# Block 1 of a retention layer computed as one chunk of 128 tokens, and no products of zeros

## The chip, the cores and the metric

The kernel runs on one core of a Trainium2 chip. The metric is the device time of one execution in microseconds (us), from three runs for the kernel before. All engine times below come from one profiled execution of that kernel.

## The reference, cut to what matters

The layer has two halves. The first is a retention (linear attention with decay) over batch 4, 8 heads, 768 tokens, head size 64, in blocks of 64 tokens. The second is a channel mix on the 512-wide result, with two weight matrices between 512 and 1024 and one gate of 512 by 512.

```python
for b in range(nb):                      # 12 blocks of 64 tokens
    intra = einsum('bhic,bhjc->bhij', qb, kb) * Dmask       # lam ** (i - j), lower triangle
    intra = einsum('bhij,bhjd->bhid', intra, vb)
    inter = einsum('bhid,bhde->bhie', qb * lam_pow, kv_state)
    out[:, :, sl] = intra + inter
    kv_state = lam_block * kv_state + einsum('bhsd,bhse->bhde', kb * rev_pow, vb)
...
xk = mu_k * x + (1 - mu_k) * x_prev ; xr = mu_r * x + (1 - mu_r) * x_prev
k = maximum(xk @ w_k, 0) ; v = k * k @ w_v ; r = sigmoid(xr @ w_r) ; return r * v
```

The block length is only a way of computing: a chunk of 128 tokens with the decay carried on gives the same numbers as two of 64.

## The kernel before, in words

The 768 tokens are cut into NT = 6 blocks of 128 (index n), and the 8 heads into HP = 4 pairs (index hp). Each step of the work is a two or three letter word, and the string `ORDER` lists all the words; every engine gets its instructions in that order, and no scheduler changes it. A word is a letter, the block and the pair (or part):

- `L` and `N` load the inputs of a block and pair on SP's queue, `M` clears the halves of the tile that must be zero (POOL). There are two input tiles, `in0` and `in1` (in_104 and in_105 where instructions are listed), for even and odd pairs, so a load waits until the pair two steps earlier has been read.
- `A` scores (PE, tile `sc`), `a` decay of the scores (DVE, into `mv`), `q` decay of the queries (DVE, also into `mv`), `k` decay of the keys (ACT), `U` sums of keys by values (PE, tile `u`), `u` and `w` the update of the state `st` (DVE, with copies by ACT), `B` values (PE, tile `xp`).
- `E`, `F`, `e`, `f` mix a token with the one before (ACT, POOL, DVE); `x`, `y` split the result in two parts (ACT, DVE); `R`, `Q` gate products (`rp`), `K` first products (`kp`), `h` and `p` square and split, `V` second products (`vp`), `s` and `o` outputs.
- `S`, `c`, `C`, `D` load a 64-bit weight matrix and turn it into 32-bit numbers (SP, ACT, POOL, DVE).
- `T` makes the tables of decay powers; `Z` followed by a count puts that many products of a zero tile on PE, into a PSUM tile `idle` that nobody reads.

Block 0 is one chunk of 128 tokens: no state is needed, 8 score products and 8 value products per pair. In every later block (n of 1 and more) each pair works on two chunks of 64, called even and odd (`eo`). There the score product has 128 rows in its stationary side, the two heads being separated by zeros, and the values are one product per head, batch and chunk: the 64 rows of values and the 64 rows of state stand on top of each other in one stationary tile, and decayed scores and decayed queries on top of each other in `mv`. That is why `to_values` copies the state into the input tile twice per pair, and why `decay_queries` writes four pieces.

In a matmul's row of the profile the two numbers with a star (128*64, 64*64) are the part of the TensorE array that it uses, rows by columns. A 32-bit product shows as two records.

Of the kernel before, what the change touches and what calls it, by code (L numbers as in the profile page):

```python
# [7 lines left out]
F32 = mybir.dt.float32  # L8
# [25 lines left out]
def tile_retention_moe(  # L34
    ctx: ExitStack,
    tc: tile.TileContext,
    qvk0: bass.AP,
# [50 lines left out]
    LP = const.tile([128, H, 64], F32, name="LP")  # L88
    LC = tiny.tile([128, HP], F32, name="LC")
# [3 lines left out]
    def load_hp(n, hp):  # L93
        t = IN[hp % 2]
        if n == 0:
            sync.dma_start(t[:, 0:4].rearrange("p c o -> p (c o)"), qvk0[hp])
            return
        sync.dma_start(t[:, 2:4].rearrange("p c o -> p (c o)"), kk[n - 1, hp])

    def load_qv(n, hp):  # L100
        t = IN[hp % 2]
        for i in range(2):
            rows, cols = slice(i * 64, i * 64 + 64), slice(i * 4, i * 4 + 2)
            sync.dma_start(t[rows, cols].rearrange("p c o -> p (c o)"), qv[n - 1, hp, rows])
# [3 lines left out]
    def clear(n, hp):  # L108
        t = IN[hp % 2]
        gpsimd.memset(t[64:128, 0 if n == 1 and hp < 2 else 1:2], 0.0)  # L110
        gpsimd.memset(t[0:64, 4 if n == 1 and hp < 2 else 5:6], 0.0)
# [6 lines left out]
    smalls = tiny.tile([128, 7 + H + 2 * HP], F32, name="smalls")  # L118
    sync.dma_start(smalls, small)
    rows = [work.tile([128, w], F32, tag="rt", name="rows", bufs=4) for w in (328, 200)]  # L120
    eye = rows[0][:, 200:328]
    sync.dma_start(rows[0], hot)
    lcol, ecol, lrow, erow, prow = (smalls[:, a:b] for a, b in ((0, 1), (1, 5), (5, 13), (13, 14), (14, 15)))
    mus = smalls[:, 7 + H:].rearrange("p (w c) -> p w c", w=2)
# [5 lines left out]
    zeros = work.tile([128, 1024], F32, tag="kf", name="zeros")  # L130
    vector.memset(zeros, 0.0)
    lone = work.tile([128, 640], F32, tag="kf", name="lone")
    gpsimd.memset(lone[:, 512:640], 1.0)
# [13 lines left out]
    rows = rows[1]  # L147
    vector.tensor_scalar(omu, mus, -1.0, 1.0, op0=ALU.mult, op1=ALU.add)
# [4 lines left out]
    idle = ps_m.tile([128, 512], F32, tag="m", name="idle")  # L153

    def powers(step):
        i = int(step[1])
        if i == 2:
            by_head = lone[:, 0:512].rearrange("p (h i) -> p h i", h=H)
            vector.tensor_tensor(by_head, rows[:, 72:136].rearrange("p (o i) -> p o i", o=1).broadcast_to([128, H, 64]),
                                 eye[:, 15::16].rearrange("p (h o) -> p h o", o=1).broadcast_to([128, H, 64]), op=ALU.mult)  # L160
            tensor.matmul(tables[2], lone[:, 512:640], lone[:, 0:512], start=True, stop=True)
            scalar.copy(LP.rearrange("p h i -> p (h i)"), tables[2])
            for ab in range(2):
                half = slice(ab * 64, ab * 64 + 64)
                gpsimd.tensor_copy(LC[half], LP[half, :, 63].rearrange("p (h a) -> p a h", a=2)[:, ab])
# [7 lines left out]
    zeros = zeros.bitcast(mybir.dt.bfloat16)  # L173

    def keep_busy(count):

        for _ in range(count):
            tensor.matmul(idle, zeros[:, 0:128], zeros[:, 512:1024], start=True, stop=True)
# [70 lines left out]
    def scores(n, hp):  # L249
        q = Q[hp % 2]  # L250
        if n == 0:
# [19 lines left out]
    def decay(n, hp):  # L271
        sc, mv = scs.pop((n, hp)), mv_of(n, hp)
        if n == 0:
# [14 lines left out]
    def decay_queries(n, hp):  # L288
        q, mv = Q[hp % 2], mv_of(n, hp)
        for eo in range(2):  # L290
            dr = slice(64, 128) if eo == 0 else slice(0, 64)
            for ab in range(2):
                rows = slice(ab * 64, ab * 64 + 64)
                lp = LP[rows, 2 * hp + ab:2 * hp + ab + 1, :].broadcast_to([64, B, 64])
                vector.tensor_tensor(mv[dr, eo, :, ab, :], q[rows, ab, :, eo, :], lp, op=ALU.mult)

    def decay_keys(n, hp):
        kn = KN[hp % 2]
        for ab in range(2):
            h = 2 * hp + ab  # L300
            scalar.activation(kn[:, :, ab, :], kn[:, :, ab, :], AF.Copy, scale=(PW if n == 0 else KD)[:, h:h + 1])

    def sums(n, hp):
        kn, vs = KN[hp % 2], VS[hp % 2]
        us[n, hp] = u = ps_1.tile([128, B, 2, 64], F32, tag="u", name="u")
        for b in range(B):
            for ab in range(2):
                if n == 0:
# [14 lines left out]

    def even_state(n, hp):
        u, state = us[n, hp][:, :, 0, :], ST[hp]
        if n == 0:
            scalar.copy(state, u)
            return
        to_values(n, hp, 0, state)
        vector.scalar_tensor_tensor(state, state, LC[:, hp:hp + 1], u, op0=ALU.mult, op1=ALU.add)  # L330
        to_values(n, hp, 1, state)

    def odd_state(n, hp):
        vector.scalar_tensor_tensor(ST[hp], ST[hp], LC[:, hp:hp + 1], us.pop((n, hp))[:, :, 1, :],
                                    op0=ALU.mult, op1=ALU.add)

    def values(n, hp):
# [146 lines left out]
Sr0 cr0 Cr0 Z10 T0 L00 Sr1 Z1 A00 k00 U00 a00 Z2 B00 cr1 L01 u00 Cr1 Sr2 k01 A01 a01 E00 U01 cr2 L02 u01 e00 T1 B01  # L484
Sr3 E01 L03 T2 F00 k02 Cr2 A02 f00 R00 e01 cr3 a02 U02 B02 M10 k03 u02 F01 f01 A03 Cr3 U03 Sk0 e02 R01 E02 a03 ck0 N10
L10 L11 Q00 f02 F02 R02 u03 Sk1 k10 q10 B03 N11 M11 Ck0 U10 E03 A10 Sk2 F03 Q01 R03 Q02 L12 e03 f03 ck1 u10 a10 B10
Sk3 N12 w10 Sv0 Sv1 M12 k11 U11 A11 s00 Ck1 Q03 s01 q11 E10 e10 ck2 k12 f10 u11 s02 K00 h00 a11 F10 A12 B11 M13 w11
L13 E11 Ck2 e11 a12 ck3 U12 K01 u12 f11 N13 K02 k13 s03 F11 Ck3 K03 w12 x10 cv0 A13 q12 B12 h01 h02 p00 h03 E12 N20
Sv2 Cv0 cv1 a13 L20 Dv0 U13 K04 u13 K05 Cv1 q13 K06 h04 p01 Dv1 K07 Sv3 M20 cv2 w13 A20 k20 U20 V00 h05 y10 L21 Cv2
k21 F12 e12 f12 V02 B13 h06 cv3 Dv2 M21 u20 Cv3 p02 N21 w20 h07 Dv3 p03 y11 x11 Dr0 V04 V06 q20 Dr1 U21 A21 V01 E13  # L490
V03 e13 V05 V07 o00 o01 a20 F13 f13 Dk0 B20 o02 o03 L22 y13 x12 R10 Q10 R11 Q11 R12 Q12 N22 u21 a21 x13 y12 Dk1 R13
Q13 L23 s10 q22 K10 s11 M22 E20 q21 K11 e20 s12 s13 w21 f20 F20 k22 U22 h10 A22 x20 Dk2 B21 K12 M23 a22 Dk3 K13 K14
h11 e21 N23 E21 F21 K15 h12 K16 p10 f21 h13 k23 u22 w22 B22 h14 U23 x21 A23 K17 p11 h15 E22 F22 u23 w23 V10 h16 y20
L30 p12 V12 a23 k30 V14 y21 e22 f22 M30 q23 h17 x22 L31 N30 A30 U30 p13 k31 B23 L32 V16 E23 V11 e23 a30 F23 u30 q30
N31 w30 V13 f23 M31 U31 y22 o10 B30 e30 u31 o11 A31 y23 k32 V15 o12 V17 R20 o13 E30 N32 q32 f30 x23 Q20 R21 Q21 R22
Q22 R23 L33 k33 Q23 q31 a31 M32 s20 w31 F30 s21 x30 B31 E31 e31 U32 F31 u32 w32 A32 a32 f31 M33 K20 s22 h20 L40 N33
K21 s23 B32 E32 F32 A33 x32 U33 h21 K22 u33 N40 q33 h22 L41 K23 h23 p20 k41 p21 K24 K25 h24 K26 K27 a33 h25 V20 k40
h26 p22 h27 y30 p23 w33 e32 f32 x31 V22 y31 V21 M40 B33 U40 A40 L42 M41 q40 e33 E33 f33 V24 u40 F33 N41 a40 w40 y32
V23 y33 B40 A41 o20 E40 U41 a41 F40 u41 V26 e40 L43 V25 V27 q41 x33 k42 o21 w41 o22 M42 f40 N42 A42 o23 B41 N43 U42
M43 L50 E41 a42 k43 u42 R30 F41 q42 w42 Q30 R31 Q31 R32 Q32 e41 R33 f41 Q33 x40 B42 s30 s31 U43 x41 A43 a43 E42 F42  # L500
q43 s32 s33 u43 w43 K30 N50 q50 x42 h30 K31 K32 h31 p30 K33 K34 h32 h33 p31 K35 h34 K36 h35 K37 L51 V30 h36 y40 e42
k50 y41 V32 V34 f42 h37 p33 p32 U50 B43 E43 A50 u50 V31 V33 y42 e43 N51 k51 F43 o30 f43 a50 q51 V35 V36 A51 U51 o31
B50 e50 a51 f50 o32 V37 E50 o33 u51 R40 Q40 F50 R41 Q41 B51 R42 Q42 x50 L52 k52 L53 x43 E51 F51 R43 y43 Q43 s40 N52
U52 N53 u52 q52 A53 s41 a53 s42 A52 K40 h40 q53 K41 h41 a52 s43 k53 K42 K43 h42 p40 K44 K45 K46 h43 h44 x51 p41 h45
e51 h46 f51 p42 K47 B52 h47 U53 y50 u53 p43 y51 V40 V42 e52 V41 E52 f52 V43 V44 F52 o40 y52 V46 V45 V47 B53 o41 o42
o43 x52 e53 f53 y53 R50 Q50 R51 Q51 R52 Q52 E53 F53 x53 R53 Q53 s50 s51 K50 K51 s52 h50 s53 h51 K52 h52 K53 h53 p51
p50 K54 h54 K55 h55 K56 K57 h56 h57 p53 V50 V52 V54 p52 V51 V53 o50 o51 V56 V55 V57 o52 o53
# [54 lines left out]
```

## Time and profile before

| what | us |
|---|---|
| median of three runs (lowest to highest) | 433.15 (430.15 to 433.55) |
| time of the profiled execution | 432.04 |
| its span from the first to the last instruction | 430.3 |
| PE busy in the span | 419.5 |
| DVE, ACT, POOL busy | 264.0, 204.9, 71.0 |
| PE's last product ends | 426.3 |

The time of the profiled execution is 1.74 us more than its span. A line of groups or of the timeline gives engine, operation, output and input tiles, the shape, a count behind an x, and in brackets the idle time of the engine ahead of it with what ended it. A line of the chain of waits gives a start, a length, and the engine that the end of the program can be traced back to in that time. A stretch of the windows view gives the busy time of each engine in it, the granted clock, the DMA share and GB/s.

### The profile page before, as it was taken

To read this page: it belongs to the slowest core of one execution; us is meant where nothing else is said; L and a number is where in the kernel's file an instruction comes from. 1 tells how busy PE (TensorE), PEld (TensorE's weight loads), DVE (VectorE), ACT (ScalarE), POOL (GpSimd) and SP (SyncE) were. 2 spreads that over 40 slices of the span, in tenths; PEclk is the share of its full clock that TensorE was granted. 3 is DMA by queue.
4 is the path that set the end of the run, shared out by engine and by line. 5 is a ranking of instruction groups with operands and counts; after the bars stand their busy time and mean duration, and the time that the engine had idled before them with its cause. 6 is when DMAs were issued, how large, how long until landed. Compare 5 with 4: busy or idle time off the path is not lost.

```text
span 430.3 us, 7314 instructions
## 1 busy us (share of the span) xinstructions
PE 419.5 (98%) x2935; PEld 328.9 (76%) x2935; DVE 264.0 (61%) x402; ACT 204.9 (48%) x357; POOL 71.0 (16%) x142
## 2 busy tenths in 40 slices
PE   7998899999999999999999999999999999999996
PEld 4665545668888888888888888888878888888885
DVE  5886999979867674746667646555437561414411
ACT  3645686586677643344644434454244460224300
POOL 4366554331102011110020200000000000000000
PEclk9999999999999999999999999999999999999999
DMA  7889918131403213515004523004520001100001
GB/s 295 304 308 330 300 48 277 66 97 50 146 3 99 87 46 107 153 58 140 0 2 131 187 78 99 0 0 123 161 62 0 2 1 50 50 2 0 0 30 69
DMA packets 12306, 42.60 MB, mean 99 GB/s; under 512 B 1776, under 2 KB 2160, under 8 KB 10736
## 3 DMA queue, kind: packets, MB, share of 16 engines
q1 hardware_dynamic: 8672, 35.84, 26.5%
q10 hardware_dynamic: 3600, 6.29, 4.0%
q8 instruction: 23, 0.38, 0.4%
q14 instruction: 11, 0.09, 0.1%
HBM read 35.83 MB, written 6.29 MB: 98 GB/s over the span
## 4 chain that ended last, share of the span: by engine, by line
PE 81%; DVE 7%; DMA 6%; ACT 2%; POOL 1%; issue 1%; SPq 0%; DVEq 0%; ACTq 0%
PE vp L30 29%; PE kp L30 26%; PE rp L30 13%; PE xp L30 5%; PE sc L30 4%; DMA wst<-w_k 4%; PE u L30 3%; DMA in<-qv 2%; DVE wst L30 2%; DVE mv L30 1%; DVE lov L30 1%; PE table L30 1%; ACT wu L30 1%; DVE wu L30 1%; POOL wu L30 1%
## 5 line engine op out<-in xcount | busy, mean ns | idle before, releaser
L30 PE MATMUL vp<-hiv,k 128*128 128x512 f32 (+1 forms) x400 | 122.8, 384 | 1.0 <-ACT kf L30 1.0
L30 PEld LDWEIGHTS vp<-hiv,k 128*128 128x128 f32 x400 | 74.1, 188 | 16.9 <-ACT kf L30 1.4
L30 PE MATMUL vp<-lov,k 128*128 128x512 f32 (+1 forms) x200 | 76.2, 381 | 0.0
L30 PE MATMUL kp<-xh,hik 128*128 128x512 f32 x160 | 62.9, 393 | 0.0
L30 PE MATMUL kp<-xl,hik 128*128 128x512 f32 x160 | 62.3, 389 | 0.0
L30 PE MATMUL kp<-xh,lok 128*128 128x512 f32 x160 | 62.3, 389 | 0.0
L30 ACT ACTIVATE ts<-xp,omu 128x512 f32<-128x512 f32 x48 | 31.8, 684 | 62.5 <-PE xp L30 44.2
L30 DVE TENSOR_TENSOR kf<-kp,kf 128x512 f32<-128x512 f32 x40 | 27.4, 688 | 37.2 <-ACT kf L30 37.1
L30 ACT ACTIVATE kf<-kp 128x512 f32<-128x512 f32 x48 | 28.4, 594 | 37.6 <-PE kp L30 37.2
L30 ACT COPY in<-st 64x256 f32<-64x256 f32 x80 | 32.3, 404 | 22.1 <-DVE st L30 17.8
L30 PEld LDWEIGHTS vp<-lov,k 128*128 128x128 f32 x200 | 37.6, 188 | 6.9
L30 DVE TENSOR_TENSOR mv<-sc,Dt 64x512 f32<-64x512 f32 (+1 forms) x48 | 32.6, 686 | 12.3 <-PE sc L30 11.9
L30 DVE TENSOR_TENSOR xl<-ts,xh 128x512 fp32r<-128x512 f32 x40 | 27.7, 703 | 19.3 <-ACT xh L30 19.2
L30 DVE SCALAR_TENSOR_TENSOR ts<-xp,smalls,ts 128x512 f32<-128x512 f32 x40 | 29.6, 747 | 15.8 <-ACT ts L30 15.6
L30 DVE TENSOR_TENSOR mv<-in,LP 64x256 f32<-64x256 f32 x80 | 34.5, 431 | 3.2 <-DMA in<-qv 1.6
L30 DVE TENSOR_TENSOR k<-kf,k 128x1024 fp32r<-128x1024 f32 x24 | 29.1, 1223 | 10.7 <-ACT k L30 10.7
L30 DVE TENSOR_TENSOR rt<-vp,rt 128x512 f32<-128x512 f32 (+1 forms) x25 | 16.4, 665 | 31.5 <-PE vp L30 31.2
L30 PEld LDWEIGHTS kp<-xh,hik 128*128 128x128 f32 x160 | 30.0, 188 | 7.0 <-issue 0.9
L30 PEld LDWEIGHTS kp<-xh,lok 128*128 128x128 f32 x160 | 30.0, 188 | 6.3
L30 PEld LDWEIGHTS kp<-xl,hik 128*128 128x128 f32 x160 | 30.0, 188 | 6.0
L30 ACT CAST xh<-ts 128x512 fp32r<-128x512 f32 x40 | 24.1, 616 | 21.7 <-DVE rt L30 18.2
L30 DVE SCALAR_TENSOR_TENSOR st<-st,LC,u 128x256 f32<-128x256 f32 x36 | 17.2, 478 | 24.8 <-ACT in L30 20.0
(70 smaller groups left out, 586.3 us busy)
## 6 DMA issues: line engine op xcount, KB each, us to landing
in<-qv SPq DMA_DIRECT2D x40, 256.0 KB, 4.5
in<-kk SPq DMA_DIRECT2D x20, 512.0 KB, 4.6
out<-rt ACTq DMA_DIRECT2D x23, 256.0 KB, 2.0
in<-qvk SPq DMA_DIRECT2D x4, 1024.0 KB, 6.3
wst<-w_k SPq DMA_DIRECT2D x4, 1024.0 KB, 9.2
wst<-w_v SPq DMA_DIRECT2D x4, 1024.0 KB, 9.7
wst<-w_r SPq DMA_DIRECT2D x4, 512.0 KB, 7.1
out<-rt ACTq DMA_DIRECT2D x2, 128.0 KB, 1.7
```

The source lines that it names most:

```text
L30: return lambda *args, **kw: self.tc.keep_in_program_order(op(*args, **kw))
```

## The change

Block 1 is computed as block 0 is: one chunk of 128 tokens per pair. Scores, sums and decay take block 0's form (`n < 2`). The state now has to come in by a product of its own: to each of the 8 value products of a pair, one product of the state with the decayed queries is added in the same PSUM place. The queries are decayed in place by one DVE instruction; the state is updated by one instruction instead of two, without the ACT copies. Queries, values and both forms of the keys of block 1 come in one DMA of 1 MB, not in one of 512 KB and two of 256 KB, and the clears of block 1 go (they come at block 2). The table `LP` covers 128 powers, by head pair, and takes the place of `LC`. The words `Z` go, with their zero tile. `ORDER` is new as a whole.

```diff
     def decay_queries(n, hp):
-        q, mv = Q[hp % 2], mv_of(n, hp)
+        q = Q[hp % 2]
+        if n == 1:
+            q = q[:, 0].rearrange("p b e i -> p b (e i)")
+            vector.tensor_tensor(q, q, LP[:, hp:hp + 1].broadcast_to([128, B, 128]), op=ALU.mult)
+            return
...
     def even_state(n, hp):
...
+        if n == 1:
+            vector.scalar_tensor_tensor(state, state, LP[:, hp, 127:128], u, op0=ALU.mult, op1=ALU.add)
+            return
...
     def values(n, hp):
-        for eo in range(1 if n == 0 else 2):
+        for eo in range(1 if n < 2 else 2):
             for b in range(B):
                 for ab in range(2):
                     rows = slice(ab * 64, ab * 64 + 64)
-                    if n == 0:
-                        tensor.matmul(xp[rows, b].rearrange("p e i -> p (e i)"), vs[:, 0, b, ab, :], mv[:, ab, b, :], start=True, stop=True)
+                    if n < 2:
+                        x = xp[rows, b].rearrange("p e i -> p (e i)")
+                        tensor.matmul(x, vs[:, 0, b, ab, :], mv[:, ab, b, :], start=True, stop=n == 0)
+                        if n == 1:
+                            tensor.matmul(x, ST[hp][rows, b], Q[hp % 2][rows, 0, b].rearrange("p e i -> p (e i)"), start=False, stop=True)
...
     for step in ORDER.split():
         if step[0] == "T":
             powers(step)
-        elif step[0] == "Z":
-            keep_busy(int(step[1:]))
...
-Sr0 cr0 Cr0 Z10 T0 L00 Sr1 Z1 A00 k00 U00 a00 Z2 B00 cr1 L01 u00 Cr1 Sr2 k01 A01 a01 E00 U01 cr2 L02 u01 e00 T1 B01
+Sr0 cr0 T0 L00 A00 L01 k00 T2 Sr1 U00 a00 B00 Sr2 Cr0 k01 A01 cr1 u00 U01 L02 E00 a01 e00 F00 T1 u01 Sr3 Cr1
```

Where the instructions stand is shown at three places. The first is the start of PE's list, ahead of the values of block 0, pair 0, as a difference (minus is before, plus is the change):

```order
-L30 LDWEIGHTS zeros
-L30 MATMUL idle<-zeros 128x512
+L557 UNCONDITIONAL_BRANCH
 L30 MATMUL table<-rows 128x64 x8
-L30 LDWEIGHTS zeros
-L30 MATMUL idle<-zeros 128x512
 L30 MATMUL sc<-in_104 128x128 x8
+L30 MATMUL table<-lone,rows 128x512
 L30 MATMUL u<-in_104 64x64 x8
```

The products of zeros are gone (ten ahead of the first table, one after it, two ahead of the values), and the third table, which stood after the values of pair 1, has come between the first scores and sums.

The second place is PE around the values of block 1, pair 0 (`xp`, with the state `st_106`). Before:

```order
L30 MATMUL rp<-wr_296,x_6_94 128x512 x2
L30 MATMUL xp<-mv,in_104 64x64 x16
L30 MATMUL u<-in_105 64x128 x8
L30 MATMUL sc<-in_105 64x128 x8
L30 MATMUL rp<-wr_296,x_7_95 128x512 x2
```

And in the change:

```order
L30 MATMUL rp<-wr_310,x_7_95 128x512 x4
L30 MATMUL sc<-in_105 128x128 x8
L30 MATMUL xp<-mv,in_104 64x128
L30 MATMUL xp<-in_104,st_106 64x128
L30 MATMUL xp<-mv,in_104 64x128
L30 MATMUL xp<-in_104,st_106 64x128
```

Sixteen products in a row of one kind have become eight of values and eight of state, which alternate one by one to the end of the pair; the output of each is 64 by 128 instead of 64 by 64.

The third place is SP's list from the last load of block 0 on. Before:

```order
L30 DMA in_105<-qvk 128x2048
L30 DMA wst<-w_k 128x2048
L30 DMA in_104<-qv 64x1024 x2
L30 DMA in_104<-kk 128x1024
L30 DMA in_105<-kk 128x1024
L30 DMA wst<-w_k 128x2048
L30 DMA in_105<-qv 64x1024 x2
```

And in the change:

```order
L30 DMA in_105<-qvk 128x2048
L30 DMA wst<-w_k 128x2048
L30 DMA in_104<-qvk 128x2048
L30 DMA wst<-w_k 128x2048 x2
L30 DMA in_105<-qvk 128x2048
L30 DMA wst<-w_k 128x2048
L30 DMA wst<-w_v 128x2048
```

The load of block 1, pair 1 now stands behind two weight blocks of 1 MB and not behind one, and as one DMA it waits for the last reader of the whole tile.

More of the change, by code (lines that the diff above doesn't have):

```diff
@@ L36, in tile_retention_moe @@
     tc: tile.TileContext,
-    qvk0: bass.AP,
+    qvk: bass.AP,
     kk: bass.AP,
@@ L87, in tile_retention_moe @@
     Dt = const.tile([128, H, 128], F32, name="Dt")
-    LP = const.tile([128, H, 64], F32, name="LP")
-    LC = tiny.tile([128, HP], F32, name="LC")
+    LP = const.tile([128, HP, 128], F32, name="LP")
     lastw = tiny.tile([128, 2, HP, B], F32, name="lastw")
@@ L94, in load_hp @@
         t = IN[hp % 2]
-        if n == 0:
-            sync.dma_start(t[:, 0:4].rearrange("p c o -> p (c o)"), qvk0[hp])
+        if n < 2:
+            sync.dma_start(t[:, 0:4].rearrange("p c o -> p (c o)"), qvk[n, hp])
             return
-        sync.dma_start(t[:, 2:4].rearrange("p c o -> p (c o)"), kk[n - 1, hp])
+        sync.dma_start(t[:, 2:4].rearrange("p c o -> p (c o)"), kk[n - 2, hp])
     def load_qv(n, hp):
@@ L103, in load_qv @@
             rows, cols = slice(i * 64, i * 64 + 64), slice(i * 4, i * 4 + 2)
-            sync.dma_start(t[rows, cols].rearrange("p c o -> p (c o)"), qv[n - 1, hp, rows])
+            sync.dma_start(t[rows, cols].rearrange("p c o -> p (c o)"), qv[n - 2, hp, rows])
     def clear(n, hp):
         t = IN[hp % 2]
-        gpsimd.memset(t[64:128, 0 if n == 1 and hp < 2 else 1:2], 0.0)
-        gpsimd.memset(t[0:64, 4 if n == 1 and hp < 2 else 5:6], 0.0)
-    smalls = tiny.tile([128, 7 + H + 2 * HP], F32, name="smalls")
+        gpsimd.memset(t[64:128, 0 if n == 2 and hp < 2 else 1:2], 0.0)
+        gpsimd.memset(t[0:64, 4 if n == 2 and hp < 2 else 5:6], 0.0)
+    smalls = tiny.tile([128, 7 + H + 3 * HP], F32, name="smalls")
     sync.dma_start(smalls, small)
-    rows = [work.tile([128, w], F32, tag="rt", name="rows", bufs=4) for w in (328, 200)]
-    eye = rows[0][:, 200:328]
+    rows = [work.tile([128, w], F32, tag="rt", name="rows", bufs=4) for w in (456, 200)]
+    eye, pair = rows[0][:, 200:328], rows[0][:, 328:456]
     sync.dma_start(rows[0], hot)
     lcol, ecol, lrow, erow, prow = (smalls[:, a:b] for a, b in ((0, 1), (1, 5), (5, 13), (13, 14), (14, 15)))
-    mus = smalls[:, 7 + H:].rearrange("p (w c) -> p w c", w=2)
+    mus = smalls[:, 7 + H:7 + H + 2 * HP].rearrange("p (w c) -> p w c", w=2)
     pows = tiny.tile([128, 7], F32, name="pows")
@@ L129, in tile_retention_moe @@
     gpsimd.memset(one, 0.0)
[L130 to L133, printed above, removed]
+    lone = work.tile([128, 512], F32, tag="kf", name="lone")
     vector.memset(rows[1][:, 0:64], 0.0)
@@ L147, in tile_retention_moe @@
     rows = rows[1]
+    vector.tensor_tensor(rows[:, 199:200], rows[:, 135:136], rows[:, 135:136], op=ALU.mult)
     vector.tensor_scalar(omu, mus, -1.0, 1.0, op0=ALU.mult, op1=ALU.add)
@@ L152, in tile_retention_moe @@
     tables = [ps_m.tile([128, 512], F32, tag="m", name="table") for _ in range(3)]
-    idle = ps_m.tile([128, 512], F32, tag="m", name="idle")
     def powers(step):
@@ L157, in powers @@
         if i == 2:
[L158 to L161, printed above, removed]
+            vector.tensor_tensor(lone.rearrange("p (h i) -> p h i", h=HP), rows[:, 72:200].rearrange("p (o i) -> p o i", o=1).broadcast_to([128, HP, 128]),
+                                 smalls[:, 7 + H + 2 * HP:].rearrange("p (h o) -> p h o", o=1).broadcast_to([128, HP, 128]), op=ALU.mult)
+            tensor.matmul(tables[2], pair, lone, start=True, stop=True)
             scalar.copy(LP.rearrange("p h i -> p (h i)"), tables[2])
-            for ab in range(2):
-                half = slice(ab * 64, ab * 64 + 64)
-                gpsimd.tensor_copy(LC[half], LP[half, :, 63].rearrange("p (h a) -> p a h", a=2)[:, ab])
             return
@@ L171, in powers @@
         scalar.copy(Dt[:, 4 * i:4 * i + 4], tables[i].rearrange("p (h x) -> p h x", h=4))
[L173 to L178, printed above, removed]
     def split(hi, lo, x):
@@ L250, in scores @@
         q = Q[hp % 2]
-        if n == 0:
+        if n < 2:
             kt = KT[hp % 2].rearrange("p b e r -> p b (e r)")
@@ L272, in decay @@
         sc, mv = scs.pop((n, hp)), mv_of(n, hp)
-        if n == 0:
+        if n < 2:
             mv = mvs[n, hp] = mv.rearrange("p e b a i -> p (e b a i)").rearrange("p (a b i) -> p a b i", a=2, b=B)
@@ L288, in decay_queries @@
     def decay_queries(n, hp):
-        q, mv = Q[hp % 2], mv_of(n, hp)
+        q = Q[hp % 2]
[3 more added lines that the diff above has]
+            return
+        mv = mv_of(n, hp)
         for eo in range(2):
@@ L293, in decay_queries @@
                 rows = slice(ab * 64, ab * 64 + 64)
-                lp = LP[rows, 2 * hp + ab:2 * hp + ab + 1, :].broadcast_to([64, B, 64])
+                lp = LP[rows, hp:hp + 1, 0:64].broadcast_to([64, B, 64])
                 vector.tensor_tensor(mv[dr, eo, :, ab, :], q[rows, ab, :, eo, :], lp, op=ALU.mult)
@@ L300, in decay_keys @@
             h = 2 * hp + ab
-            scalar.activation(kn[:, :, ab, :], kn[:, :, ab, :], AF.Copy, scale=(PW if n == 0 else KD)[:, h:h + 1])
+            scalar.activation(kn[:, :, ab, :], kn[:, :, ab, :], AF.Copy, scale=(PW if n < 2 else KD)[:, h:h + 1])
     def sums(n, hp):
@@ L307, in sums @@
             for ab in range(2):
-                if n == 0:
+                if n < 2:
                     tensor.matmul(u[ab * 64:ab * 64 + 64, b, 0], kn[:, b, ab, :], vs[:, 0, b, ab, :],
@@ L328, in even_state @@
             return
+        if n == 1:
+            vector.scalar_tensor_tensor(state, state, LP[:, hp, 127:128], u, op0=ALU.mult, op1=ALU.add)
+            return
         to_values(n, hp, 0, state)
-        vector.scalar_tensor_tensor(state, state, LC[:, hp:hp + 1], u, op0=ALU.mult, op1=ALU.add)
+        vector.scalar_tensor_tensor(state, state, LP[:, hp, 63:64], u, op0=ALU.mult, op1=ALU.add)
         to_values(n, hp, 1, state)
     def odd_state(n, hp):
-        vector.scalar_tensor_tensor(ST[hp], ST[hp], LC[:, hp:hp + 1], us.pop((n, hp))[:, :, 1, :],
+        vector.scalar_tensor_tensor(ST[hp], ST[hp], LP[:, hp, 63:64], us.pop((n, hp))[:, :, 1, :],
                                     op0=ALU.mult, op1=ALU.add)
@@ L483 @@
 ORDER = """
-Sr0 cr0 Cr0 Z10 T0 L00 Sr1 Z1 A00 k00 U00 a00 Z2 B00 cr1 L01 u00 Cr1 Sr2 k01 A01 a01 E00 U01 cr2 L02 u01 e00 T1 B01
[L485 to L507, printed above, removed]
+Sr0 cr0 T0 L00 A00 L01 k00 T2 Sr1 U00 a00 B00 Sr2 Cr0 k01 A01 cr1 u00 U01 L02 E00 a01 e00 F00 T1 u01 Sr3 Cr1
@@ new lines @@
+B01 f00 L03 R00 E01 cr2 F01 k02 A02 U02 u02 e01 a02 Cr2 cr3 R01 B02 A03 Sk0 L10 Sk1 f01 Q00 Cr3 e02 k03 E02 a03 ck0
+Sk2 U03 u03 Q01 F02 k10 f02 A10 q10 Ck0 U10 B03 E03 F03 R02 e03 Q02 R03 a10 L11 ck1 Q03 s00 s01 f03 A11 Sk3 B10 Ck1
+s02 K00 Sv0 q11 L12 ck2 a11 e10 K01 Sv1 k11 u10 E10 Ck2 F10 U11 f10 B11 ck3 k12 A12 s03 h00 E11 u11 Ck3 x10 h01 cv0
+p00 U12 a12 Sv2 Cv0 L13 e11 K02 K03 K04 h02 h03 F11 cv1 f11 Dv0 p01 Sv3 L20 Cv1 K05 h04 q12 x11 K06 K07 A13 k20 h05
+cv2 Dv1 y10 a13 q13 k13 B12 u12 E12 V00 e12 F12 h06 U13 f12 B13 M20 N20 V02 Cv2 u13 U20 h07 A20 L21 p02 N21 cv3 M21
@@ new lines @@
+y11 Dv2 k21 V04 u20 Cv3 w20 E13 e13 p03 V06 A21 Dv3 Dr0 f13 a20 U21 L22 V01 L23 V03 F13 y13 x12 Dr1 o00 V05 q20 V07
+Dk0 k22 o01 B20 o02 R10 o03 Q10 R11 a21 y12 x13 u21 M22 e20 Q11 Dk1 R12 N22 f20 Q12 w21 R13 Q13 s10 q21 s11 E20 K10
+F20 Dk2 A22 s12 x20 B21 h10 U22 a22 N23 s13 Dk3 K11 q22 h11 K12 E21 h12 u22 F21 k23 e21 w22 K13 h13 K14 K15 M23 p10
+f21 h14 h15 L30 K16 U23 p11 B22 x21 u23 M30 A23 q23 K17 h16 k30 V10 V12 V14 w23 N30 E22 a23 y20 h17 U30 L31 F22 e22
+A30 f22 y21 B23 p13 p12 V11 u30 E23 k31 q30 a30 V13 V16 N31 x22 V15 w30 o10 q31 y22 F23 e23 f23 V17 B30 o11 A31 L32
@@ new lines @@
+o12 M31 o13 N32 E30 U31 R20 Q20 k32 R21 e30 f30 F30 a31 Q21 A32 M32 u31 B31 w31 L33 M33 y23 U32 x23 u32 a32 R22 E31
+k33 q32 Q22 N33 w32 R23 Q23 s20 K20 F31 A33 e31 L40 f31 s21 U33 s22 x31 s23 L41 x30 u33 B32 h20 K21 q33 h21 K22 K23
+K24 N40 h22 h23 p20 p21 h24 w33 k40 E32 K25 a33 h25 K26 h26 F32 q40 K27 V20 M40 V22 A40 h27 y30 e32 U40 f32 B33 y32
+M41 y31 p22 p23 x32 V24 e33 E33 f33 L42 V21 V23 F33 N41 a40 u40 B40 A41 w40 k42 q41 k41 U41 E40 V26 e40 V25 F40 o20
+u41 V27 w41 a41 N42 f40 L43 y33 o21 M42 U42 A42 o22 u42 o23 q42 B41 R30 Q30 w42 R31 e41 x33 a42 E41 F41 k43 f41 N43
@@ new lines @@
+Q31 R32 Q32 R33 s30 s31 Q33 s32 A43 B42 N50 L50 M43 U43 u43 w43 x40 L51 q43 K30 a43 s33 K31 K32 h30 h31 K33 p30 h32
+x41 h33 K34 h34 q50 K35 h35 k50 p31 E42 F42 p32 K36 K37 y40 h36 e42 V30 k51 f42 h37 p33 y41 U50 x42 A50 B43 V32 V31
+u50 V34 e43 a50 E43 F43 f43 N51 U51 A51 q51 y43 B50 L52 V36 o30 y42 a51 e50 f50 k52 V33 V35 E50 u51 N52 F50 o31 U52
+A52 x43 B51 o32 V37 E51 o33 R40 Q40 R41 Q41 R42 F51 Q42 R43 Q43 s40 s41 s42 K40 h40 K41 h41 s43 K42 K43 h42 p40 e51
+f51 N53 K44 K45 K46 u52 h43 h44 p41 a52 h45 h46 p42 K47 h47 y50 p43 q53 q52 L53 x50 V40 y51 V42 V41 V43 x51 V44 A53
@@ L508 @@
+a53 k53 B52 U53 u53 e52 E52 f52 F52 o40 y52 V46 V45 V47 B53 o41 o42 o43 x52 e53 f53 y53 R50 Q50 R51 Q51 R52 Q52 E53
+F53 x53 R53 Q53 s50 s51 K50 K51 s52 h50 s53 h51 K52 h52 K53 h53 p51 p50 K54 h54 K55 h55 K56 K57 h56 h57 p53 V50 V52
+V54 p52 V51 V53 o50 o51 V56 V55 V57 o52 o53
 """
@@ L526, in reverse @@
         x = x[..., ::-1, :]
-        return np.concatenate([x[:, :, :, :1, ::-1], x[:, :, :, 1:]], axis=3)
+        return np.concatenate([x[:, :, :, :2, ::-1], x[:, :, :, 2:]], axis=3)
     by_column = (3, 1, 2, 6, 0, 4, 5)
@@ L533 @@
     arrays = {
-        "qvk0": np.stack([x[0] for x in parts], axis=2).reshape(HP, 128, 2048),
-        "kk": np.concatenate([x[1:] for x in parts[2:]], axis=3),
-        "qv": np.concatenate([x[1:] for x in parts[:2]], axis=3),
+        "qvk": np.stack([x[:2] for x in parts], axis=3).reshape(2, HP, 128, 2048),
+        "kk": np.concatenate([x[2:] for x in parts[2:]], axis=3),
+        "qv": np.concatenate([x[2:] for x in parts[:2]], axis=3),
         "small": np.concatenate([
@@ L544 @@
             moe_mu_r.reshape(HP, 128).T,
+            np.repeat(np.eye(HP, dtype=np.float32), 32, axis=0),
         ], axis=1),
-        "hot": np.concatenate([np.tile(np.eye(200, dtype=np.float32)[191:63:-8], (H, 1)), np.eye(128, dtype=np.float32)], axis=1),
+        "hot": np.concatenate([np.tile(np.eye(200, dtype=np.float32)[191:63:-8], (H, 1)), np.eye(128, dtype=np.float32),
+                               np.tile(np.kron(np.eye(2, dtype=np.float32), np.outer(np.arange(16) == 15, np.ones(64)).astype(np.float32)), (HP, 1))], axis=1),
         "w_r": moe_w_r.view(np.int64).reshape(4, 128, 512),
```

2 lines of the change are left out of this document (1 added, 1 removed).

## The prediction

> **What bounds the kernel now.** I read the totals first, then PE's waits, then the span cut where PE stops waiting, and only then single rows.
>
> ```profile
> span 430.3 us, 7314 instructions
> PE 419.5 (98%) x2935; PEld 328.9 (76%) x2935; DVE 264.0 (61%) x402; ACT 204.9 (48%) x357; POOL 71.0 (16%) x142
> ```
>
> PE is busy all but 10.8 us. The windows say where that is (columns: stretch, its length, PE, PEld, DVE, ACT, POOL, clock, DMA share, GB/s):
>
> ```profile
> 0.00:6.70 6.70, 4.45 (x10) 1.31 (x10) 3.69 (x13) 2.15 (x3) 4.72 (x10) 1.00 0.66 219
> 6.70:32.24 25.54, 25.03 (x261) 17.83 (x263) 20.99 (x36) 14.28 (x28) 10.95 (x21) 1.00 0.87 325
> 32.24:93.04 60.80, 56.83 (x392) 33.27 (x388) 52.06 (x66) 42.15 (x73) 32.50 (x33) 1.00 0.62 194
> 93.04:426.30 333.26, 333.21 (x2276) 276.54 (x2276) 186.20 (x290) 146.33 (x255) 22.79 (x80) 1.00 0.20 62
> 426.30:430.30 4.00, 0.00 (x0) 0.00 (x0) 1.02 (x2) 0.00 (x0) 0.00 (x0) 0.99 0.27 98
> ```
>
> After 93.04 PE does not pause until its last product at 426.30. Before that, its waits are few, and the view of PE's waits has all of them:
>
> ```profile
> PE idle L30 <- DVE zeros L30: 2.0, 1, 2.0
> PE sc L30 <- DMA in<-qv: 1.6, 1, 1.6
> PE xp L30 <- DVE mv L30: 1.4, 1, 1.4
> PE vp L30 <- ACT kf L30: 1.0, 1, 1.0
> PE sc L30 <- DMA in<-qvk: 0.5, 1, 0.5
> PE table L30 <- DVE rows L30: 0.3, 1, 0.3
> ```
>
> So from the first table at 6.71 on, the time is PE's work plus 4.5 us of waits (1.6, 1.4, 1.0, 0.5). The 2.0 and the 0.3 lie ahead of the first table, which needs the DVE chain of powers, and that chain is kept. **Work saved on DVE, ACT or POOL is worth at most these waits; work added on PE counts in full.** The question is what the change adds on PE.
>
> **The values of block 1: what one product costs when the shape changes.** Two triples from the chain of waits, both outside the change, carry the main term:
>
> ```profile
> 126.68 1.02 PE u L30 x16
> 127.71 0.87 PE sc L30 x16
> 128.58 0.93 PE xp L30 x32
> ...
> 304.18 1.02 PE sc L30 x16
> 305.20 0.61 PE u L30 x16
> 305.81 1.08 PE xp L30 x32
> ```
>
> In the first triple all three groups use the array as 128*64, and only the first, which follows 128*128 products, shows 1.02; the same kind of group after an equal shape takes 0.87, and `xp` 0.93. In the second, the last block's sums use 64*64. Then `xp` after them takes 1.08. So a **change of shape costs 0.15 us** (1.02 less 0.87; 1.08 less 0.93). The timeline at that place shows what happens:
>
> ```profile
> 304.92 0.28 PE L30 MATMUL sc<-in 128*64 128x128 f32 x2
> 305.13 0.68 PE L30 MATMUL u<-in 64*64 64x64 f32 x16
> 305.74 1.15 PE L30 MATMUL xp<-mv,in 128*64 128x64 f32 x32
> ```
>
> The last two score records, one in each column half of the array, both start at 304.92. The next shape starts 0.21 us later, when neither is streaming any more, although a pair of records in an even run follows the last pair after 0.109 us (0.87 us for 16 records, two side by side). Within one shape, then, the two halves work side by side; across a change of shape the trace has nothing side by side.
>
> In the change, each pair's values alternate a product 128*64 (values) with one 64*64 (state): 16 products, each another shape than its neighbours. Alone, a product of 128 columns is two records one after the other, 2 x 0.109 = 0.218, plus the change, 0.15: 0.37 us. Sixteen make 5.9 us per pair. Before, it is 0.93 to 1.08, so 1.0. Four pairs: 4 x (5.9 - 1.0) = **+19.6 us**. The bounds of this unknown: if the two shapes mix freely, all 32 records run at 0.054 and the pair costs 32 x 0.054 + 0.15 = 1.9 us (+3.6 in all); if a state product can run beside the other head's value product but each couple must end first, eight couples of 0.37 make 3.0 us (+8.0). I take the upper end, since every change of shape that the trace shows is of that kind.
>
> [...]
>
> **Sums and scores of block 1.** They take block 0's form, whose rows are in the chain:
>
> ```profile
> 10.96 0.54 PE idle L30 x2
> ...
> 12.64 1.12 PE sc L30 x16
> 13.77 0.61 PE u L30 x16
> ```
>
> Sums go from 0.87 to 1.02 down to 0.61: 4 x (0.61 - 0.95) = -1.3. Scores go from 0.87 to 1.02 up to about 1.10: 4 x 0.15 = +0.6.
>
> **What goes on the other engines.** Per pair, from the groups:
>
> ```profile
> L30 DVE TENSOR_TENSOR mv<-in,LP 64x256 f32<-64x256 f32 x80 | 34.5, 431 | 3.2 <-DMA in<-qv 1.6
> L30 ACT COPY in<-st 64x256 f32<-64x256 f32 x80 | 32.3, 404 | 22.1 <-DVE st L30 17.8 <-PE u L30 1.2 <-POOL in L30 1.2
> L30 DVE SCALAR_TENSOR_TENSOR st<-st,LC,u 128x256 f32<-128x256 f32 x36 | 17.2, 478 | 24.8 <-ACT in L30 20.0 <-PE u L30 4.2
> L30 DVE TENSOR_TENSOR mv<-sc,Dt 128x512 f32<-128x512 f32 x8 | 5.1, 685 | 2.5 <-PE sc L30 2.5
> L30 DVE TENSOR_TENSOR lone<-rows 128x512 f32<-128x512 f32 x1 | 0.8, 824 | 0.0
> ```
>
> DVE loses four query pieces (4 x 0.431) and one state update (0.478), and gains one 128x512 product, between 0.685 and 0.824 by the last two rows: about -1.45 us a pair, -5.8 in all. ACT loses four copies, -1.6 a pair. None of it is on PE's path by itself. It ends the waits: with 52.06 of 60.80 us DVE is the fullest engine behind PE in the stretch of the waits 1.4 and 1.0, and the copies and the query pieces stand in just that chain of DVE and ACT. The wait of 1.6 is for a query load of block 1; the new order has the values of pair 0 and two groups `kp` ahead of that place. So I take the 4.5 us off, and the 0.5 that PE covers with two products of zeros ahead of the first values (row at 10.96): there it waits for `mv`, and in the change the third table stands in that gap. Together **-5.0**; the least is 0, if each wait returns elsewhere. What is late next is the load below.
>
> **The products of zeros.**
>
> ```profile
> 1.98 4.45 PE L30 MATMUL idle<-zeros 128*128 128x512 bf16 x10 [1.98 <-DVE zeros L30]
> 6.71 2.10 PE L30 MATMUL table<-rows 128*128 128x64 f32 x16 [0.28 <-DVE rows L30]
> 8.95 1.16 PE L30 MATMUL sc<-in 64*128 64x128 f32 x16
> ...
> 12.60 1.16 PE L30 MATMUL sc<-in 64*128 64x128 f32 x16
> ```
>
> All thirteen lie in time in which PE had nothing else: taking them away frees nothing. But they do something. Ten in 4.45 us is one each 0.43 us, while products of the same 512 columns later come every 0.23:
>
> ```profile
> 129.51 13.82 PE kp L30 x60
> ```
>
> So they ran at half speed (the clock column says 1.00 there, so it does not show this), and by 8.95 the scores take the same 1.16 as at 12.60: the full clock came between 6.4 and 8.95, that is 4.4 to 7.0 us after PE's first work. Without zeros that slow time starts at the first table: half of it is lost, 2.2 to 3.5 us, less what PE would have waited there anyway; the cost is between 0 and 3.5. [...]
>
> **The load of block 1, pair 0.** One DMA of 1 MB now, which waits for the values of block 0, pair 2, the last reader of `in0`.
>
> ```profile
> 19.99 1.98 PE L30 MATMUL rp<-wr,x 128*128 128x512 f32 x4
> 22.42 1.04 PE L30 MATMUL xp<-mv,in 128*64 128x128 f32 x16
> ...
> 24.73 2.60 SPq L30 DMA_DIRECT2D in<-kk  x2
> ...
> 30.25 0.91 ACT L30 ACTIVATE in<-in,KD 128x256 f32<-128x256 f32 x2 [3.81 <-DMA in<-kk]
> ```
>
> Before, those values end at 23.5 and the keys of block 1 land at 30.25, behind 7.6 MB issued earlier (block 0, `w_r` and the first of `w_k`); the bytes ahead are the same in the change, so about 30.3 again. There, PE has between those values and the first scores of block 1 one score group (1.1), one sum group (0.6) and two `rp` pairs (2 x 1.8): 5.3 us. With the values' end near 24, PE stands at those scores at about 29.5 and waits 0.9. Behind them, in order, stand the sums, the values of pair 3 and the remaining gate products. This wait swallows part of the clock's loss, and the loss part of it: together I take **+2.0** (0 to 4).
>
> **The sum,** against the profiled execution: 432.0 + 19.6 - 1.3 + 0.6 - 5.0 + 2.0 = **448** us. That execution lies 1.1 us under the median of 433.15, so the change would be 3.4% slower than the median. One measurement of this kernel cannot tell less than about 1% from no change.
>
> **The rivals.** (1) *State products run beside value products of the other head*, ended couple by couple: +8.0 in place of +19.6, **436 us**. For it: the halves are independent within one shape. Against it: no row shows two shapes at once. (2) *The shapes mix freely*, 1.9 us a pair: +3.6, **432 us**. This one is not slower: it decides from 1.9 us a pair down, where the removed waits pay for the added product, and with nothing added for the clock it would come to 430. For it speaks the even run of 0.054 us a record; against it every change of shape. (3) *The order at the start holds PE up more*: the slow clock pushes the values of pair 2, these push the load, the load the rest, and the waits of 4.5 us come back: up to +7 on the forecast, **455 us**. Against it: at the 219 and 325 GB/s of the first two windows, the 7.6 MB issued ahead of that load keep the DMA engines busy until about 25.5, so a small delay moves no landing. (4) *The zeros' removal alone gives time back*: not possible beyond the 0.5 already counted, by the rows above.
>
> **How the numbers follow.** Forecast 448 (444 to 452): 0.62. Rival 1: 0.14. Rival 2: 0.17. Rival 3: 0.07. The range leaves out most of rival 2 and rival 3: 434 to 452. Slower by over 1% (above 437.5): the forecast and rival 3, with a little of rival 1, 0.70. Within 1%: most of rival 1 and of rival 2, 0.25. Faster: the rest of rival 2 with no loss at the start, 0.05.
>
> **What would show it.** In the profile of the change, a block 1 value group of about 5.9 us in PE's timeline, with starts 0.2 us apart at each change of shape (3.0 means rival 1, 1.9 rival 2); sums of 0.61; PE without a wait after about 31 us; first table and first scores slower than 2.10 and 1.16; a wait of about 1 us for `qvk` at the first scores of block 1. I am wrong if two shapes run side by side, or if PE waits later for something that the new order has put too late.

## The result, and the profile after

| kernel | median us | lowest to highest | runs |
|---|---|---|---|
| before | 431.65 | 430.02 to 433.55 | 4 |
| the change | 447.11 | 446.78 to 447.98 | 4 |

The ratio is 1.036, with a 95% interval from 1.030 to 1.042: the change makes the kernel slower by about 15 us. In the experiments below, three executions were slow (850.77 and 437.10 us of the kernel before, 1592.80 of the same without its zeros), and the ratios leave them out. The profiled execution of the change took 446.78 us, with a span of 445.0. Its page opens with these rows:

```profile
span 445.0 us, 7213 instructions
PE 434.0 (98%) x2922; PEld 337.0 (76%) x2922; DVE 253.8 (57%) x386; ACT 199.4 (45%) x341; POOL 64.4 (14%) x131
```

PE works 14.5 us longer, DVE 10 us less, ACT 5.5 less. PE's 419.5 us of before hold 4.45 us of zero products ahead of the first table, so its other work has grown by more than 14.5. The windows view, cut at the same kind of places as before (stretch, length, PE, PEld, DVE, ACT, POOL, clock, DMA share, GB/s):

```profile
0.00:6.97 6.97, 0.00 (x1) 0.00 (x1) 2.79 (x11) 2.16 (x3) 4.62 (x10) 1.00 0.67 231
6.97:32.28 25.31, 25.31 (x226) 17.93 (x226) 17.52 (x31) 13.57 (x27) 7.39 (x15) 1.00 0.77 301
32.28:100.75 68.47, 68.47 (x366) 36.01 (x365) 43.26 (x52) 37.04 (x56) 26.97 (x26) 1.00 0.44 169
100.75:441.03 340.28, 340.25 (x2332) 283.07 (x2332) 189.23 (x292) 146.67 (x256) 25.41 (x82) 1.00 0.21 63
```

From the first table at 6.97 to the last product at 441.03 PE stands still for 0.03 us in all. The view of PE's waits has one row left, the start:

```profile
PE table L30 <- DVE rows L30: 7.0, 1, 7.0
```

So every wait of before is gone, and the time is 15 us longer all the same. The chain of waits (start, length, engine and output) shows where it went; the rows of block 1 and of the start:

```profile
6.97 3.68 PE table L30 x16
10.65 2.01 PE sc L30 x16
12.66 1.45 PE table L30 x2
...
43.09 5.77 PE xp L30 x32
...
55.93 0.62 PE u L30 x16
56.54 5.62 PE xp L30 x32
62.17 1.09 PE sc L30 x16
...
85.77 5.77 PE xp L30 x32
...
95.12 5.62 PE xp L30 x32
```

The values of block 1 take 5.62 to 5.77 us for a pair. PE's timeline before has these four groups:

```profile
39.99 1.41 PE L30 MATMUL xp<-mv,in 128*64 128x64 f32 x32 [1.35 <-DVE mv L30]
51.20 1.13 PE L30 MATMUL xp<-mv,in 128*64 128x64 f32 x32
64.55 1.10 PE L30 MATMUL xp<-mv,in 128*64 128x64 f32 x32
87.95 1.15 PE L30 MATMUL xp<-mv,in 128*64 128x64 f32 x32
```

The groups behind them start 1.41, 0.93, 0.93 and 1.08 us after these starts, so a pair now takes about five times as long. (A row's length runs past the start of the next group, 1.13 against 0.93 us at 51.20; starts are the safer measure.) PE's timeline inside one of the new groups:

```profile
43.02 0.43 PE L30 MATMUL xp<-mv,in 128*64 128x128 f32 x2
43.38 0.43 PE L30 MATMUL xp<-in,st 64*64 64x128 f32 x2
43.74 0.43 PE L30 MATMUL xp<-mv,in 128*64 128x128 f32 x2
```

Each product (two records) starts 0.36 us after the one ahead of it, and no two start together: 16 x 0.36 = 5.8.

### The profile page after: what moved, and what is told of

Its sections match the earlier page's. It is cut to its first block, busy times and chain, and to the rows that moved or that the text cites. A ratio compares the mean times of both kernels' runs of the same rounds, so it can differ in the third digit from the quotient of the medians.

```text
span 445.0 us, 7213 instructions
## 1 busy us (share of the span) xinstructions
PE 434.0 (98%) x2922; PEld 337.0 (76%) x2922; DVE 253.8 (57%) x386; ACT 199.4 (45%) x341; POOL 64.4 (14%) x131
## 4 chain that ended last, share of the span: by engine, by line
PE 98%; DVE 1%; DMA 1%; DVEq 0%; issue 0%; SPq 0%
PE kp L30 31%; PE vp L30 30%; PE rp L30 16%; PE xp L30 9%; PE sc L30 6%; PE u L30 4%; PE table L30 2%; DMA rows<-hot 1%; DVE rows L30 1%; DVEq L557 0%; DVE rt L30 0%; SPq L30 0%; DVE pows L30 0%; DVEq L30 0%
## 5 line engine op out<-in xcount | busy, mean ns | idle before, releaser
L30 ACT COPY in<-st 64x256 f32<-64x256 f32 x64 | 25.9, 405 | 49.4 <-DVE st L30 24.7
L30 DVE SCALAR_TENSOR_TENSOR st<-st,LP,u 128x256 f32<-128x256 f32 x32 | 15.3, 478 | 45.2 <-ACT in L30 28.0
L30 PE MATMUL xp<-mv,in 128*64 128x64 f32 (+1 forms) x640 | 35.9, 235 | 0.0
L30 DVE TENSOR_TENSOR xl<-ts,xh 128x512 fp32r<-128x512 f32 x40 | 26.9, 688 | 10.0 <-ACT xh L30 9.8
L30 PEld LDWEIGHTS xp<-mv,in 128*64 128x64 f32 x640 | 26.4, 137 | 7.3 <-issue 6.2
```

The source lines that it names most:

```text
L30: return lambda *args, **kw: self.tc.keep_in_program_order(op(*args, **kw))
```

## The experiments: what makes the group long

The theory, the author's reading of the 0.21 us between two shapes at 304.92 in the trace of before, is that each change of shape lets the array run empty. Its rivals: that a state product adds onto sums which the product just ahead has written, or that 64*64 products are slow by themselves. The four kernels below are the change with another order of the products inside block 1's value group, or, in the twin, with other products there. Their edits are shown in short form: `own` is the value product and `carried` the state product of the kernel's loop. The kernel before measured 430.89 us in the same session (13 runs).

**All value products, then all state products.** Of each head's products in a pair only the first starts a new sum, and the last closes it.

```diff
-for b in range(B):
-    for ab in range(2):
-        own(b, ab)          # value product, starts the sum
-        carried(b, ab)      # state product, adds to it
+for b, ab in every: own(b, ab)
+for b, ab in every: carried(b, ab)
```

> The change, but in block 1 a pair's eight value products come first and its eight state products behind them: one change of shape inside the group instead of fifteen. Theory (each change of shape makes the array run empty): the group of 5.62 to 5.77 us falls to two even runs of 0.87 us and two changes of 0.15, about 2.0 us; four pairs give 4 x 3.7 = 14.8 us back, so 447.1 less 14.8 is 432.3, or up to 435 if waits that the long groups covered come back. Rival (what costs is that a state product adds onto sums that the product just ahead of it has written, shape or not): the same fall, since the two are eight products apart here. Rival (64*64 products of 128 columns are slow by themselves, 0.36 us each): the group stays over 3.7 us and the time over 439.

Measured: 434.01 us (433.06 to 435.29, 10 runs); ratio to before 1.006, from 1.003 to 1.009. In its timeline:

```profile
44.17 1.09 PE L30 MATMUL xp<-mv,in 128*64 128x128 f32 x16
45.20 1.09 PE L30 MATMUL xp<-in,st 64*64 64x128 f32 x16
46.22 7.13 PE L30 MATMUL kp<-x,wk 128*128 128x512 f32 x16
```

The group takes 2.05 us, the same 32 records that took 5.77. Eight 64*64 products of 128 columns take 1.02, as fast as the value products, so they are not slow by themselves. 13 us are back. The other rival is still in. One wait that the long groups covered has returned: 1.0 us ahead of the values of pair 1, for a mix on DVE.

**By batch: two value products, two state products.**

```diff
-    for ab in range(2):
-        own(b, ab)
-        carried(b, ab)
+    for ab in range(2): own(b, ab)
+    for ab in range(2): carried(b, ab)
```

> The change, but the order inside a group is by batch: the value products of both heads, then the state products of both. Eight runs of two products side by side, so half the changes of shape. Theory: two records of 0.109 one after the other in each column half, plus 0.15, is 0.37 us for a run of two; eight make 2.95 us, so 4 x 2.75 = 11 us less than the change, about 436. If the cost were per product and not per change of shape, the group would stay near 5.7 us.

Measured: 436.07 us (one run). The chain has 2.94, 3.01, 2.94 and 2.79 us for the four groups:

```profile
43.45 2.94 PE xp L30 x32
...
54.14 3.01 PE xp L30 x32
```

Half the changes, half the time: two products side by side and one change take 0.37 us, and one product and one change took 0.36. The cost hangs on the change of shape, not on the product.

**The same shape twice.** The state product is replaced by the value product once more, onto the same sums; block 1 then lacks the state.

```diff
-        carried(b, ab)
+        own(b, ab)          # again, adds onto what it has just written
```

> The change, but each state product is replaced by the value product ahead of it, once more, added onto the same sums: equal shapes all along (the state is left out of block 1, so this computes something else). Theory: 32 records in an even run, 32 x 0.054 + 0.15 = 1.9 us per group, about 432 in all. Rival (adding onto sums just written is what costs): the group stays at 5.6 to 5.8 us and the time at 447.

Measured: 436.02 us (one run). Its chain:

```profile
57.10 1.99 PE xp L30 x32
...
82.69 1.95 PE xp L30 x32
...
88.19 1.80 PE xp L30 x32
```

1.8 to 2.0 us a group, with each product adding onto the sums of the one just ahead: adding shows no cost beside the 2.05 us of the grouped kernel. The total is 4 us over what was expected, for reasons outside the group: PE waited 2.0 us for loads of `qvk` and 1.1 us for a mix on DVE, and the slow start lasted longer than in the change (the values of block 0, pair 0, begin at 15.73 in the chain, against 14.72).

**Shapes in turn, sums apart.** The state product behind each value product belongs to a sum two batches away.

```diff
-        own(b, ab)
-        carried(b, ab)
+    for i in range(8):
+        own(*every[i])
+        carried(*every[(i + 4) % 8])
```

> The change, but the state product behind a value product belongs to another batch, two batches away, so that no product adds onto sums that the one ahead of it has written; the shapes still alternate one by one. Theory: nothing changes, the group stays at 5.6 to 5.8 us and the time at 447. Rival (adding onto sums just written is what costs): the group falls to 1.9 to 3.0 us and the time to 432 to 436.

Measured: 447.55 us (one run), and groups as long as in the change:

```profile
43.85 5.77 PE xp L30 x32
...
57.31 5.62 PE xp L30 x32
```

This and the twin settle it. With equal shapes and dependent sums the group takes 1.9 us; with alternating shapes and independent sums it takes 5.7. The twin, by batch and apart kernels have one execution each, so their times are rough; the argument rests on the lengths of the groups.

## The experiments: the start

With the groups in order, 3 us over the kernel before were left, and the first table, scores and third table of the change are 3.68, 2.01 and 1.45 us. The kernel before measured 430.59 us in the session of the next four kernels and 430.67 in that of the last two.

**Ten products of zeros in front again,** in the change as it is.

```diff
-Sr0 cr0 T0 L00 ...
+Sr0 cr0 Z10 T0 L00 ...
```

> The change with ten products of zeros ahead of the first table, as before. Theory (they bring TensorE to full speed before the real work): the first table goes from 3.68 back to 2.1 us, the first scores from 2.0 to 1.1, the third table from 1.45 to 1.1, together 2.9 us; the load of block 1, pair 0 then shows as a wait at its first scores of up to 1.5 us, since its landing is set by the bytes ahead. Time 444 to 446 against 447.1. Rival (the start has slack anyway, so the slow stretch costs nothing in the end): 447.

Measured: 447.62 us (445.02 to 449.08, 4 runs): not the 444 to 446 expected, and no gain that can be told. Its timeline and its windows (the clock is the column behind POOL) show why:

```profile
1.98 4.15 PE L30 MATMUL idle<-zeros 128*128 128x512 bf16 x10 [1.98 <-DVE zeros L30]
6.96 2.00 PE L30 MATMUL table<-rows 128*128 128x64 f32 x16 [0.83 <-DVE rows L30]
9.04 2.04 PE L30 MATMUL sc<-in 64*128 64x128 f32 x16
```

```profile
6.90:9.00 2.10, 2.00 (x16) 1.86 (x16) 1.18 (x5) 0.00 (x0) 0.17 (x1) 1.00 1.01 414
9.00:11.00 2.00, 1.96 (x16) 1.75 (x16) 0.00 (x0) 1.39 (x3) 0.00 (x0) 0.53 0.97 406
11.00:13.00 2.00, 2.00 (x10) 0.70 (x10) 1.79 (x4) 0.09 (x1) 0.00 (x0) 0.62 0.85 348
```

The table runs at full speed (2.00 us, granted clock 1.00), then the clock is taken back: 0.53 from 9 to 11 us and 0.62 from 11 to 13. If it was half while it was down, these two means make it an estimated (0.47 x 2 + 0.38 x 2) / 0.5 = 3.4 us. The scores take 2.04 again. Loads that PE now reached sooner cost 2.2 us more in waits.

**The kernel before without its zeros.**

```diff
-Sr0 cr0 Cr0 Z10 T0 L00 Sr1 Z1 A00 k00 U00 a00 Z2 B00 ...
+Sr0 cr0 Cr0 T0 L00 Sr1 A00 k00 U00 a00 B00 ...
```

> The kernel before with its thirteen products of zeros left out and nothing else. Theory: nothing is gained where they stood, the first products run at half speed for some 6 us and lose 2 to 3 us there, and 4.5 us of waits later on (for loads, and for DVE) take part of that back: between no change and +2.9 us, I expect about +1 to +2. Rival (zeros only take time): 0.5 to 1 us faster.

Measured: 433.14 us against 430.59, ratio 1.0056 (1.0036 to 1.0077). The zeros are worth about 2.5 us there (1.6 to 3.3 by the interval), more than the 1 to 2 expected and inside the stated bounds of 0 to 2.9; nothing came free by dropping them.

**Grouped values and ten products of zeros.**

```diff
-for ... : own(b, ab); carried(b, ab)
+for b, ab in every: own(b, ab)
+for b, ab in every: carried(b, ab)
...
-Sr0 cr0 T0 L00 ...
+Sr0 cr0 Z10 T0 L00 ...
```

> The grouped values and the ten products of zeros together. Theory: 434.0 for the grouped version less 2.9 for the start, plus waits that PE's lateness covered: the load of block 1, pair 0 (up to 1.5) and the mix of pair 0 ahead of the values of pair 1 (1.0 already in the grouped version, DVE-bound): 432 to 433.5, level with the kernel before (430.9) to within 1%. Rival (waits have no part in it any more): 431.

Measured: 432.23 us (12 runs), ratio 1.0043 (1.0010 to 1.0076), as expected. In its profile the clock is taken back as with the ten zeros above (0.51 and 0.64 from 9 to 11 and from 11 to 13 us), and the wait for the mix is still there, 1.0 us.

**The same, and the mix of block 1, pair 0 earlier on DVE.**

```diff
-... u10 E10 Ck2 F10 U11 f10 B11 ...
+... u10 E10 F10 f10 Ck2 U11 B11 ...
```

> The grouped values and the zeros, and on DVE the mix of block 1, pair 0 (two instructions, 1.4 us) ahead of the conversion of the third block of w_k, not behind it. Theory: the values of pair 1 wait for that mix, which waits for the conversion and its load; moved ahead, the wait of 1.0 us or more before those values goes and nothing else takes its place, since the conversion is needed only four products later: 1 to 2 us less than with the zeros alone, 430 to 432. Rival (another wait of the same size stands behind it): no difference between the two.

Measured: 431.85 us (12 runs), ratio 1.0021 (0.9993 to 1.0048). Against the version with the mix behind, the intervals overlap: the gain of 1 to 2 us was not seen. In its profile the wait for the mix is gone, and one of 1.3 us for a load of `qvk` has come, at the first scores of block 1; whether the one took the place of the other cannot be told, since the two profiles also differ at the start. In its profiled execution the ten zeros ran and the first table was slow nevertheless:

```profile
1.98 4.45 PE L30 MATMUL idle<-zeros 128*128 128x512 bf16 x10 [1.98 <-DVE zeros L30]
6.76 3.67 PE L30 MATMUL table<-rows 128*128 128x64 f32 x16 [0.33 <-DVE rows L30]
10.37 2.08 PE L30 MATMUL sc<-in 64*128 64x128 f32 x16
```

**The mix earlier, and no zeros** (grouped values throughout).

```diff
-Sr0 cr0 Z10 T0 L00 ...
+Sr0 cr0 T0 L00 ...
```

> Grouped values with the mix of block 1, pair 0 ahead of the conversion of w_k's third block, and no products of zeros. Theory: the 1.0 us wait of the grouped version before the values of pair 1 goes: 434.0 less 1.0, about 433.0. Rival (another wait of the same size stands behind it): 434.

Measured: 433.52 us, ratio 1.0071 (1.0058 to 1.0083). That lies halfway between the theory (433.0) and the rival (434), and the interval overlaps that of the grouped version (1.003 to 1.009), so the times decide nothing. The two profiles say more. The values of pair 1 in the grouped version, and here:

```profile
54.95 1.09 PE L30 MATMUL xp<-mv,in 128*64 128x128 f32 x16 [0.99 <-DVE ts L30]
54.30 1.05 PE L30 MATMUL xp<-mv,in 128*64 128x128 f32 x16
```

The wait is gone, and no other has come in its place. The values of pair 0 begin 0.5 us later than in the grouped version (44.68 against 44.17): the first table starts at 7.15 in place of 6.98, and full speed came later too (the values of block 0, pair 0, at 15.68, still took 1.58 us, against 1.04 in the change). The values of pair 1 begin 0.65 us earlier. So the wait did go, and in these two profiles the later start hides part of the gain.

**Zeros that do not stop.** Grouped values, the mix earlier, twelve zero products in front, and one of 256 columns behind each of the first table's eight products.

```diff
+            if i == 0:
+                tensor.matmul(idle[:, 0:256], zeros[:, 0:128], zeros[:, 512:768], start=True, stop=True)
...
-Sr0 cr0 Z10 T0 L00 ...
+Sr0 cr0 Z12 T0 L00 ...
```

> Grouped values, mix first, and zeros that do not stop: twelve products ahead of the first table and one of 256 columns behind each of its eight products. [...]

Measured: 430.92 us (429.96 to 432.46, 12 runs), ratio 0.9992 (0.9967 to 1.0017): level with the kernel before. The author had expected 430 to 432 if the scores and the third table take 1.1 us each, and 433 to 434 if the scores stay at 2.0. Its timeline after the table:

```profile
9.36 1.16 PE L30 MATMUL sc<-in 64*128 64x128 f32 x16
10.45 1.13 PE L30 MATMUL table<-lone,rows 128*128 128x512 f32 x2
```

Scores and third table take 1.16 and 1.13 us, and the granted clock is 1.00 from 6.9 to 15 us, at the price of a 2.4 us table (2.00 in the change with ten zeros). PE then waits 2.2 us for loads. No version beats the kernel before by more than its measurement can tell: grouped values still add 3.8 us to PE over the old ones (4 x 2.05 less 4.35).

## Why the prediction was right

It said 448 us, and 447.11 was measured. Term by term, in the two profiled executions:

- Values of block 1: +19.6 was forecast, from 5.9 us a group. From start to start, the four groups took 23.0 us where the old ones took 4.35 (1.41, 0.93, 0.93 and 1.08): +18.6. The step that carried it, a change of shape at 0.15 us with nothing side by side, is shown by the grouped, by-batch, twin and apart kernels, not only argued. A product alone between two changes took 0.36 us, against 1.02 us for eight in an even run. Rivals 1 and 2, with 3.0 and 1.9 us a group, are out.
- Sums and scores: -1.3 and +0.6 forecast; 0.61 or 0.62 and 1.09 each, as said.
- Waits: -5.0 forecast (4.5 of waits and 0.5 for two zero products), and none is left.
- The start: +2.0 was forecast for the clock and a load wait together. It came out as the slow start alone: from the first table to the sums, the steps are 2.6 us longer than the same steps before, and the table starts 0.26 later (the chain of waits now begins with the load into `rows`, 2.70 us, which has grown from 328 to 456 columns). The slow stretch lasted from 6.97 into the third table (12.66 to 14.11), so some 6 to 7 us, at the upper end of the 4.4 to 7.0 us read from the zeros. That fit is partly luck. A first table takes 2.00 us at full speed (ten zeros in front of the change) and 3.67 slow (the mix earlier); the kernel before took 2.10, so its full speed came, by the author's estimate, between 6.4 and 7.0 us, 4.4 to 5.0 after PE's first work at 1.98. And in the grouped kernel, with the same start as the change, the sums at 14.67 still took 1.05 us in place of 0.61, so its slow stretch, from 6.98 on, lasted some 7.7 us at the least. The granted clock reads 1.00 over the whole start of the change, so only the pace of the products shows the slow stretch (scores 2.01 us, later ones 1.09); that it is the clock is the author's reading, since the scores take as long, 2.04 us, where the clock reads 0.53, in the change with ten zeros. The loss differs from one execution to the next.
- The load: its wait did not come, and two figures behind it were wrong. PE was not at the first scores of block 1 at 29.5, worked out without the slow stretch, but at 32.28. The load did not land at 30.3 but shortly before 31.69, when ACT took the keys: with the values of pair 2 later, it was issued at 26.9 and not at 24. The argument against rival 3, that the bytes ahead keep the DMA engines busy and a small delay moves no landing, did not hold: with the load of pair 2 of block 0 issued at 15.69 in place of 12.73, the DMA share from 13 to 15 us was 0.02 (0.69 before). No wait came of it, since PE was later still.
- The zeros: that removing them frees nothing was right, by the kernel before without them. What that part missed is that the clock can be taken back after full speed (0.53 from 9 to 11 us in the change with ten zeros, behind a table of 2.00 us).
- The sum: from the first table to the last product PE worked 434.03 us against 415.07 (sums of the windows), 19.0 more. Less the 4.5 of waits and plus the 0.26 this makes 14.7, which is the difference of the two profiled executions (446.78 less 432.04). The forecast had 16.0: the values were put 1.0 too high and the start 0.9 too low, so these two errors nearly cancel; the rest is spread over groups that were not forecast one by one.

## What to carry to other kernels

Small products of two array shapes should stand in runs, not in turn: one change cost more here than a product of 128 columns in an even run (0.15 against 0.109 us), and nothing in a count of products shows it, while two neighbouring groups in a profile (0.87 against 1.02) do. On a kernel whose PE hardly stops, as this one, relief for other engines (10 us on DVE, 5.5 on ACT) was worth only PE's waits, and the profile gave their sum beforehand (4.5 us). Before dropping work that seems idle, look at whether the first real products behind it run at full speed (here the first table took 2.10 us with zeros ahead, 3.68 without).

## What the runs showed of the hardware that was not expected

The granted clock went back to 0.53 and 0.62 (means from 9 to 11 and from 11 to 13 us; an estimated 3.4 us at half speed, by the sum above) after a gap of only 0.83 us and 2.0 us of 64-column products, although PE had not been idle for longer since its first product. Two profiles show it: the change with ten zeros, and the grouped values with ten zeros (0.51 and 0.64, after a gap of 0.87 us). With denser zeros in the same place it stayed at 1.00; there the gap was 0.41 us and a zero product stood behind each product of the table, and which of the two did it was not separated. Ten products of zeros gave three different starts: slow zeros and a fast table in the kernel before (4.45 and 2.10 us), a fast table and slow scores (2.00 and 2.04 us, in the change with ten zeros), or slow zeros and a slow table (4.45 and 3.67 us, with the mix earlier). What decides between them was not tested.
